# First pair's casts to GpSimd and copies to ScalarE, gate halves in two PSUM banks, and a newly listed order, in a block-sparse attention and MLP-mixer kernel

## Chip, cores, metric

One core of a Trainium2 chip. The metric is the device time in microseconds (us) of one execution, the median of several runs. Engines are named as in the profile: PE (TensorE), DVE (VectorE), ACT (ScalarE), POOL (GpSimd), SP (SyncE, here used only to issue DMAs).

## The reference

```python
# q, k, v: (4, 8, 768, 64) float32; block 64, so 12 blocks; top_k 3
k_rep = k.reshape(B, H, 12, 64, D).mean(axis=3)
gate  = einsum('bhsd,bhnd->bhsn', q, k_rep), -1e9 where the block lies in the future
# each query attends to the 3 best blocks and to its own block, causally
attn  = softmax(where(mask & causal, q @ k^T / 8, -1e9)) @ v
x  = attn as (B, S, 512)
h  = relu(x^T @ w_tok1) @ w_tok2 ;  u = x + h^T          # token mixing, 768 -> 256 -> 768
out = u + relu(u @ w_ch1) @ w_ch2                         # channel mixing, 512 -> 1536 -> 512
```

Inputs and output are float32; the kernel computes scores, attention and the MLP in float16 and the gate in float32.

## The kernel before, in words

The 32 heads are worked in 16 pairs, four pairs to a batch (`pair(p)`, p = 0 to 15), and after each batch's pairs stands its channel MLP (`mlp(b)`). For a pair:

- q and k are loaded ("k<-in_k_dram", "q<-in_q_dram", line 516; q from pair 6 on and k from pair 7 on in another layout, line 508), transposed on PE (line 446) or, later, on DVE (lines 539, 596). v is loaded by a DMA that POOL issues and that casts to float16 ("VA", line 525), as are the weights ("w", "wc", line 426).
- From the transposed k, DVE sums blocks (line 553, tile "ks") and `spread` (line 534) copies the sums to the two heads' places. PE multiplies them with the transposed q (line 639: the gate), DVE adds the causal bias (643), takes the top 8 (670), compares with the third (683) and clears the own block (690, tile "bn"). "bn" is transposed by PE (710) and stands as 12 further rows under q (tile "QA"), so that one matmul gives score and mask (731, tile "sc").
- QA's upper rows are q cast to float16; KA's are k cast to float16 (lines 342 and 344: `copy` on ACT, and on DVE or POOL).
- ACT takes the exponent (744, tile "E"), POOL clears the upper triangle (752), PE multiplies with v (761), DVE divides (764, 768). Token mixing follows: 779, 783 or 784, 793, 796, and u is transposed, on PE (807) for the first four pairs, and later by DVE and a trip through DRAM ("turn", lines 452, 456, 460). The channel MLP is lines 827 (first matmul), 835 and 837 (relu), 849 (second matmul), 853 and the store.

The first pair (`cut`, p < CUT = 1) is worked in two halves of the sequence, so that it can start when half of its data is there: its transposes, gates, "bn" and scores come in two parts.

The order of every engine's instructions is fixed while the kernel is recorded. `Plan` holds all steps with their costs by engine (in ns), their dependences and a priority each (`pr`, from the numbers in `L`); `Plan.run` lists them greedily, and also decides which engine takes a step that several could take. Each engine then runs its list strictly in order. Where the plan sees PE wait, `fill` puts in matmuls of zeros (line 899) until the first MLP step. Costs for DMAs are (issue, landing, transfer); `LANES` = 8 is how many SP and ACT transfers may be under way. `P.alone` names the PSUM rings whose tiles are used by one engine at a time: a step of another engine on the same tile waits for the earlier one.

Of the kernel before, what the change touches and what calls it, by code (L numbers as in the profile page):

```python
# [51 lines left out]
EARLY, PACE = 5.78, 16.48  # L52
L = dict(kd=28.39, qd=24.29, vd=11.04, kt=13.4, kr=28.62, ke=-12.17, qt=24.03, qe=-10.99, q16=7.68, g=11.64, b=22.27,
         k16=20.14, r=24.99, w1=-9.34, w2=-3.8, wc1=11.98, wc2=30.18, tok=11.05, ml=12.98, o0=-2.69, o1=2.1, o2=2.23,
         o3=-0.75, o4=-2.45, o5=-0.39, o6=-3.33, o7=-8.31, o8=-1.83, o9=0.42, o10=-4.09, o11=-5.38, o12=6.03,
         o13=-1.8, o14=0.66, o15=3.06, m0=-0.25, m1=4.0, m2=6.99, m3=2.31, th=5.48, bd=5.16, cu=0.88, cs=5.86,
         ua=3.23, ub=23.41, ku=26.38, k0=5.54, k1=3.72, qu=23.81, dq=5.5, qp=5.5, dk=6.49, va=-11.68, ekd=26.02,
         eqd=24.07, evd=9.12, ekt=15.03, ekr=34.55, eke=-11.24, eqt=24.03, eqe=-6.62, eq16=4.03, eg=11.13, eb=22.27,
         etok=17.72)
# [28 lines left out]
class Plan:  # L88
# [6 lines left out]
    DMA = 1.1  # L95
# [33 lines left out]
    def run(self, on_slot_end=None, fill=None):  # L129
        free = dict(FREE)  # L130
        dma_free, lanes = 0.0, [0.0] * self.LANES
# [30 lines left out]
        def start(o, e):  # L162
            t = max(free[e] + held(o, e), o.not_before)
            if ported(o, e):
                t = max(t, shared[0])
            if e in ("SP", "ACT") and len(o.cost[e]) > 2:
                t = max(t, lanes[0])
# [23 lines left out]
        while ready:  # L191
# [47 lines left out]
            if len(o.cost[e]) > 2:  # L239
                begin = max(dma_free, t + occ)  # L240
                dma_free = begin + o.cost[e][2] * self.DMA
                o.end = dma_free + lat
                if e != "POOL":
                    lanes.pop(0)
                    lanes.append(o.end)
# [54 lines left out]
def kernel(  # L300
# [122 lines left out]
    def weight(name, dst, src, n, each, pr, after):  # L423
        b = Buf(None)
        W[name] = (b, 0)
        P.op({"POOL": (800.0, 2200.0, n * each / 16.0)}, lambda: nc.gpsimd.dma_start(out=dst, in_=src), rd=[after], wr=[(b, 0)], pr=pr)

    def weights(after):
        weight("w1", w1, moe_w_tok1.rearrange("(j p) t -> p j t", p=128), 768, 60, L["w1"], after)
        weight("w2", w2, moe_w_tok2.rearrange("(g p) s -> p g s", p=128), 256, 135, L["w2"], after)  # L430
        for c in range(NCC):
            weight(("wc1", c), wc1[:, c, :], moe_w_ch1[128 * c:128 * c + 128, :], 128, 247, L["wc1"] + c, after)
        for f in range(0, NFC, 3):
            weight(("wc2", f), wc2[:, f:f + 3, :], moe_w_ch2[128 * f:128 * f + 384, :].rearrange("(g p) c -> p g c", p=128),
                   384, 98, L["wc2"] + f / 3, after)
# [46 lines left out]
    def pair(p):  # L482
# [38 lines left out]
        if p < 3:  # L521
# [3 lines left out]
        P.op({"POOL": (1100.0, 2200.0, 1536 * 16.0 / 16)}, lambda: nc.gpsimd.dma_start(  # L525
            out=VA.t[:, :, :, 0:64], in_=vs.rearrange("x (j p) d -> p x j d", p=128)), wr=[(VA, 0)], pr=t0 - lead["vd"], not_before=5000.0)

# [4 lines left out]
        def spread(e, z):  # L532
            for x in range(2):
                ENG[e].tensor_copy(out=ks2b.t[64 * x:64 * x + 64, x, z], in_=ks3.t[64 * x:64 * x + 64, 0, z])  # L534

        if straight_k:
# [6 lines left out]
            for x in range(2):  # L543
                P.op({"POOL": (772.0, 820.0), "ACT": (721.0, 825.0), "DVE": (470.0, 555.0)}, lambda e, x=x: copy(ENG[e], KA.t[0:64, x, :], KT.t[64 * x:64 * x + 64]),
                     port=True, rd=[(KT, 0), (KT, 1)], wr=[(KA, (x, 0)), (KA, (x, 1))], io=f"S{2 * x}>S0", pr=t0 - lead["ke"])
            if not thirds:
                P.op({"POOL": (380.0, 450.0), "DVE": (160.0, 240.0)}, lambda e: spread(e, slice(0, NB)), rd=[(ks3, 0), (ks3, 1)], wr=[(ks2b, 0), (ks2b, 1)], pr=t0 - lead["kr"] + 0.1, io="S0>S0 S2>S2")
        else:
            k16 = Buf(k16r)
            for i in range(2):  # L550
                t = Buf(Rr)
                P.op(pe(slow=3), lambda t=t, i=i: transposed(k32, i, t.t), rd=loaded(k32, i), wr=[(t, 0)], pr=at(i, lead["kt"]))
                P.op(dve(HS), lambda t=t, i=i: nc.vector.tensor_reduce(  # L553
                    out=ks3.t[:, 0, 6 * i:6 * i + 6], in_=t.t[:, 0:HS].rearrange("c (n w) -> c n w", w=64),
                    axis=AX.X, op=ALU.add), rd=[(t, 0)], wr=[(ks3, i)], io="P0>S0", pr=at(i, lead["kr"]))
                if not thirds and (cut or i == 1):
                    z = slice(6 * i, 6 * i + 6) if cut else slice(0, NB)
                    P.op({"POOL": (380.0, 450.0), "DVE": (160.0, 240.0)}, lambda e, z=z: spread(e, z), rd=[(ks3, i)] if cut else [(ks3, 0), (ks3, 1)],
                         wr=[(ks2b, i)] if cut else [(ks2b, 0), (ks2b, 1)], pr=at(i, lead["kr"]) + 0.1, io="S0>S0 S2>S2")
# [34 lines left out]
        for i in range(2):  # L594
# [9 lines left out]
            P.op({**act(HS), **dve(HS)}, qev, rd=[(t, 0)], wr=[(QT, i)], io="P0>S0", pr=at(i, lead["qe"]))  # L604
# [5 lines left out]
        if straight_q and thirds:  # L610
            P.op({"POOL": (1207.0, 1257.0), "DVE": (745.0, 828.0)}, lambda e: ENG[e].tensor_tensor(
                out=R1.t, in0=QT.t[:, 128:S], in1=upper(QT.t[:, 128:S]), op=ALU.subtract), port=True, rd=[(QT, 0), (QT, 1)], wr=[(R1, 0), (R1, 1)], io="S0>S0", pr=t0 - L["r"])
# [14 lines left out]
        g = Buf(Rr)  # L627
        gm, m8, bn = Buf(gmr), Buf(m8r), Buf(bnr)
        W2 = 2 * NB
        if not thirds:  # L630
            if cut:
                P.op({"POOL": (100.0, 150.0)}, lambda: nc.gpsimd.memset(gm.t[:, 0:2].rearrange("p j (x n) -> p j x n", n=NB)[:, :, :, 6:NB], -1.0e9), wr=[(gm, 9)], pr=t0 - lead["g"] - 9.0)
            for i, (z0, z1) in enumerate(parts):
# [3 lines left out]
                def gate(z0=z0, z1=z1, nb=nb):  # L637
# [4 lines left out]
                P.op(pe(slow=2 * (z1 - z0)), gate, rd=both_q + [(ks2b, 0)] + ([(ks2b, 1)] if z1 > 2 else []), wr=[(g, i)], pr=at(i, lead["g"]))  # L642
                P.op({"DVE": (200.0 * (z1 - z0) / 5 + 40.0 * cut, 290.0)}, lambda z0=z0, z1=z1, nb=nb, cols=cols: nc.vector.tensor_tensor(
                    out=cols(gm.t[:, z0:z1]), in0=g.t[:, W2 * z0:W2 * z1].rearrange("p (j w) -> p j w", w=W2)[:, :, 0:2 * nb].rearrange("p j (x n) -> p j x n", n=nb),
                    in1=cols(gbias[:, z0:z1]), op=ALU.add), rd=[(g, i)] + ([(gm, 9)] if cut else []), wr=[(gm, i)], io="P0S0>S0", pr=at(i, lead["g"]) + 0.1)
        else:
# [11 lines left out]
            for i in range(3):  # L658
                P.op({"DVE": (202.0, 283.0)}, lambda i=i: nc.vector.tensor_tensor(out=gm.t, in0=gv(2 - i), in1=(gm.t if i else gbias), op=ALU.add),
                     rd=[(g, 0)], wr=[(gm, 0)], io="P0S0>S0", pr=t0 - lead["g"] + 0.1)  # L660

        for i, (z0, z1) in enumerate(parts):
# [8 lines left out]
            P.op({"DVE": (730.0 * nz / 5, 730.0 * nz / 5 + 90.0)}, top, rd=[(gm, i)], wr=[(m8, i)], io="S0>S0", pr=at(i, lead["g"]) + 0.2)  # L671
            nb = 6 if cut and i == 0 else NB
            if thirds:
                P.op({"DVE": (92.0, 174.0)}, lambda z0=z0, z1=z1, third=third: nc.vector.tensor_copy(out=third(), in_=m8.t[:, z0:z1, :, 2:3]),
                     rd=[(m8, i)], wr=[(g, (3, i))], io="S0>P0", pr=at(i, lead["g"]) + 0.25)
                pair_of = lambda: (gm.t.rearrange("p j (x n) -> p j x n", n=NB), third())
            else:
                pair_of = lambda z0=z0, z1=z1, nb=nb: (
# [5 lines left out]
            P.op({"DVE": (190.0 * sm, 190.0 * sm + 82.0)}, less, rd=[(gm, i), (g, i), (g, (3, i)), (m8, i)], wr=[(bn, i)], io="P0S0>S0", pr=at(i, lead["g"]) + 0.3)  # L684
# [6 lines left out]
            P.op({"POOL": (270.0, 340.0), "DVE": (150.0, 220.0)}, mine, rd=[(bn, i)], wr=[(bn, i)], io=">S0 >S2", pr=at(i, lead["g"]) + 0.4)  # L691
# [251 lines left out]
```

## Time and profile before

| what | value |
|---|---|
| median of 3 runs | 246.92 us (246.72 to 247.88) |
| profiled execution | 246.32 us, span 244.6 us |
| granted TensorE clock | 1.0 |
| busy: PE, DVE, ACT, POOL | 97%, 70%, 66%, 52% of the span |
| DMA packets | 30.82 MB, mean 126 GB/s |
| first channel-MLP matmul on the chain | at 56.46 us |

The span is the profiled program's time on the core; 1.72 us of the execution lie around it. In lists of groups a line reads: line, engine, operation, output <- input, count, busy us, mean ns. In the timeline a row is start, duration, engine, line, operation, shapes, and in brackets the idle time before it and what ended it. Chain rows are start, duration, and whose work it was. In the kernel after, the same lines have numbers higher by 13 to 19.

### The profile page before, as it was taken

The numbers are of one execution on the slowest core, as the hardware profiler recorded it, in microseconds if no ns is written. First come the engines' busy times: TensorE is split into PE (matmuls) and PEld (weight loads), VectorE is DVE, ScalarE is ACT, GpSimd is POOL, SyncE is SP. The second block draws the span as 40 slices with busy tenths as digits, with TensorE's granted clock in tenths as the row PEclk, the third lists the DMA queues.
The fourth block names the chain that finished last, engine by engine and source line by source line (L and its number), as shares of the span: only waits on it lengthen the run. The fifth ranks groups of instructions, "written<-read, shape, count | busy, mean of one in ns | idle before, by whom it ended". The sixth has DMA issues, their size and how long they took to land.

```text
span 244.6 us, 6642 instructions
## 1 busy us (share of the span) xinstructions
PE 238.1 (97%) x2467; PEld 162.9 (67%) x2467; DVE 170.4 (70%) x546; ACT 160.6 (66%) x251; POOL 128.2 (52%) x263
## 2 busy tenths in 40 slices
PE   7799999999999999999999999999999999999995
PEld 7588878897656676567575666567755766554644
DVE  3889887877879999999999889968385632202112
ACT  3786978759587696788988675589724672360620
POOL 6188778878487583978796747676102110000000
DMA  8999999999899897879999899510213211112103
GB/s 158 201 203 215 207 171 182 173 132 177 133 83 168 158 148 142 186 150 178 161 138 168 186 166 126 151 53 3 64 46 111 79 32 46 43 43 86 46 18 110
DMA packets 124120, 30.82 MB, mean 126 GB/s; under 512 B 117652, under 2 KB 120596, under 8 KB 124088
## 3 DMA queue, kind: packets, MB, share of 16 engines
q1 hardware_dynamic: 94400, 22.89, 46.7%
q0 software_dynamic: 28064, 7.08, 32.8%
q10 hardware_dynamic: 1624, 0.43, 0.9%
q8 instruction: 19, 0.31, 0.6%
q14 instruction: 13, 0.11, 0.2%
HBM read 29.01 MB, written 8.45 MB: 153 GB/s over the span
## 4 chain that ended last, share of the span: by engine, by line
PE 91%; DMA 3%; DVE 3%; issue 0%; SPq 0%; POOL 0%; POOLq 0%
PE pm L827 26%; PE pm L849 25%; PE sc L731 14%; PE pm L761 9%; PE pm L779 4%; PE pm L793 4%; DMA k<-in_k_dram 3%; PE pm L639 2%; PE pm L654 2%; PE pm L446 2%; PE pm L710 1%; PE pm L899 1%; DVE ks L553 1%; DVE ks L534 1%; PE pm L807 1%; DVE m L670 1%
## 5 line engine op out<-in xcount | busy, mean ns | idle before, releaser
L744 ACT ACTIVATE E<-sc 128x1024 f16<-128x1024 f32 (+2 forms) x96 | 84.0, 917 | 22.7 <-PE sc L731 21.3
L827 PE MATMUL pm<-uT,wc 128*128 128x384 f16 x384 | 69.9, 326 | 0.0
L849 PE MATMUL pm<-wc,h 128*128 128x512 f16 (+2 forms) x312 | 68.8, 363 | 0.0
L752 POOL TENSOR_SCALAR_AFFINE_SELECT E<-E 128x256 f16<-128x256 f16 (+1 forms) x96 | 39.2, 416 | 43.2 <-ACT E L744 41.4
L835 ACT ACTIVATE h<-pm 128x384 f16<-128x384 f32 x71 | 34.5, 491 | 28.2 <-PE pm L827 28.0
L827 PEld LDWEIGHTS <-wc 128*128 128x128 f16 x384 | 36.0, 98 | 22.5
L731 PE MATMUL sc<-QA,KA 76*128 76x512 f16 (+3 forms) x264 | 48.2, 301 | 0.3 <-DVE QA L344 0.3
L849 PEld LDWEIGHTS <-h 128*128 128x128 f16 x312 | 28.4, 98 | 26.0
L853 DVE TENSOR_TENSOR os<-u,pm 128x512 f32<-128x512 f16 (+2 forms) x26 | 16.6, 640 | 33.9 <-PE pm L849 33.2
L731 PEld LDWEIGHTS <-KA 76*128 76x128 f16 x264 | 23.6, 98 | 14.5 <-issue 0.4
L761 PEld LDWEIGHTS <-E 128*128 128x128 f16 x672 | 24.9, 98 | 3.6
L761 PE MATMUL pm<-VA,E 128*128 128x65 f16 x672 | 26.1, 193 | 0.0
L796 DVE TENSOR_TENSOR u<-x,pm 128x384 f16<-128x384 f16 x32 | 16.5, 542 | 4.7 <-PE pm L793 4.7
L837 DVE TENSOR_SCALAR h<-pm 128x384 f16<-128x384 f32 x25 | 13.8, 554 | 8.5 <-PE pm L827 7.5
L768 DVE TENSOR_TENSOR x<-pm,rc 128x384 f16<-128x384 f32 x32 | 17.8, 555 | 0.9
L525 POOL DMA_DIRECT2D VA<-in_v_dram x16 | 16.8, 1051 | 0.4 <-issue 0.3
L793 PE MATMUL pm<-h,w 128*128 128x128 f16 x192 | 13.8, 219 | 0.0
L342 ACT COPY QA<-bnt 12x384 f16<-12x384 f16 x20 | 10.2, 508 | 5.3 <-DVE bnt L695 4.9
L670 DVE MAX8 m<-gm 128x8 f32<-128x12 f32 x160 | 13.2, 156 | 0.5
L779 PE MATMUL pm<-x,w 128*128 128x128 f16 x192 | 13.3, 219 | 0.0
L793 PEld LDWEIGHTS <-w 128*128 128x128 f16 x192 | 11.9, 98 | 1.9
L779 PEld LDWEIGHTS <-w 128*128 128x128 f16 x192 | 11.7, 98 | 2.0 <-DVE x L768 0.4
(79 smaller groups left out, 302.2 us busy)
## 6 DMA issues: line engine op xcount, KB each, us to landing
out_dram<-os SPq DMA_DIRECT2D x22, 256.0 KB, 2.5
q<-in_q_dram SPq DMA_DIRECT2D x42, 96.0 KB, 2.9
k<-in_k_dram SPq DMA_DIRECT2D x38, 96.0 KB, 3.8
VA<-in_v_dram POOLq DMA_DIRECT2D x16, 192.0 KB, 6.0
wc<-in_moe_w_ch_dram POOLq DMA_DIRECT2D x8, 384.0 KB, 6.6
k<-in_k_dram SPq DMA_DIRECT2D x12, 192.0 KB, 5.6
turn<-k SPq DMA_DIRECT2D x11, 192.0 KB, 2.1
uT<-turn SPq DMA_DIRECT2D x44, 48.0 KB, 2.0
```

Of the source, the lines that this page charges most:

```text
L525: P.op({"POOL": (1100.0, 2200.0, 1536 * 16.0 / 16)}, lambda: nc.gpsimd.dma_start(out=VA.t[:, :, :, 0:64], in_=vs.rearrange("x (j p) d -> p ...
L731: nc.tensor.matmul(out=s.t[:, at:at + 128 * m], lhsT=KA.t[:, x, 128 * kk:128 * kk + 128], rhs=QA.t[:, q0:q0 + m, x, :], start=True, stop=True)
L744: nc.scalar.activation(out=E.t[:, BASE[g_]:BASE[g_ + 1]], in_=s.t[:, 0:WIDTH[g_]], func=AF.Exp, scale=scale)
L752: nc.gpsimd.affine_select(out=o, in_=o, pattern=[[0, len(d)], [1, 128]], compare_op=ALU.is_ge, fill=0.0, base=0, channel_multiplier=-1)
L761: nc.tensor.matmul(out=t[:, jq, :], lhsT=E.t[:, cc:cc + 128], rhs=VA.t[:, x, kk, :], start=(kk == 0), stop=(kk == jq))
L768: P.op(dve(384), lambda a=a, rc=rc, x=x: nc.vector.tensor_tensor(out=xp.t[:, :, 64 * x:64 * x + 64], in0=a.t[:, 0:NJ * 65].rearrange("p (j ...
L779: nc.tensor.matmul(out=m1.t[:, 128 * t:128 * t + 128], lhsT=w1[:, j, 128 * t:128 * t + 128], rhs=xp.t[:, j, :], start=(j == 0), stop=(j == ...
L793: nc.tensor.matmul(out=m.t[:, 128 * j:128 * j + 128], lhsT=w2[:, t, 128 * (j0 + j):128 * (j0 + j) + 128], rhs=h1.t[:, t, :], start=(t == 0 ...
L827: nc.tensor.matmul(out=m.t[:, 0:HS], lhsT=wc1[:, c, 128 * f:128 * f + 128], rhs=uT.t[:, c].rearrange("p (a w) -> p a w", a=4)[:, :, 96 * i ...
L835: nc.scalar.activation(out=o, in_=w, func=AF.Relu)
L849: nc.tensor.matmul(out=m.t[:, 0:wide], lhsT=h2.t[:, f, 128 * jj:128 * jj + 128], rhs=wc2[:, f, w:w + wide], start=(f == 0), stop=(f == NFC ...
L853: P.op(dve(wide), lambda j=j, m=m, o=o, w=w, wide=wide: nc.vector.tensor_tensor(out=o.t[:, w:w + wide].rearrange("p (c d) -> p c d", d=128 ...
```

## The change

For the first pair: q's casts to QA go to POOL alone (before: DVE or ACT), k's copies to KA and q's copies out of PSUM to ACT alone (before: DVE or ACT). The two halves of its gate get a PSUM bank each (`gs`), before they shared one. Its v load is issued only after the second half of q is transposed (`rd=[(QT, 1)]`); for other pairs the v load stands later in the text but waits for nothing new. `spread` on DVE is now a reduction over one element instead of a copy. The plan's costs are changed: some DVE costs up, the port rule for DVE and POOL taken away for several copies, POOL's transfers given a time of preparation and a queue of their own that pushes transfers already sent, and DMAs issued after 13 us with a full queue 1.3 us more. The numbers in `L` and `EARLY` are new, a key `kr1` is added, and with all this every engine's list is another.

```diff
-EARLY, PACE = 5.78, 16.48
+EARLY, PACE = 5.56, 16.48
...
-    DMA = 1.1
+    DMA = 1.05
+    PREPARE, BEHIND = 1200.0, 1300.0
...
             if len(o.cost[e]) > 2:
-                begin = max(dma_free, t + occ)
-                dma_free = begin + o.cost[e][2] * self.DMA
-                o.end = dma_free + lat
-                if e != "POOL":
+                span = o.cost[e][2] * self.DMA
+                if t > 13000.0 and dma_free > t + 500.0:
+                    lat += self.BEHIND
+                if e == "POOL":
+                    begin = max(cast_free, t + occ + self.PREPARE)
+                    cast_free = begin + span
+                    o.end = cast_free + lat
+                    for x in sent:
+                        if x.end - 1600.0 > begin:
+                            x.end += span
...
-        P.op({"POOL": (1100.0, 2200.0, 1536 * 16.0 / 16)}, lambda: nc.gpsimd.dma_start(
-            out=VA.t[:, :, :, 0:64], in_=vs.rearrange("x (j p) d -> p x j d", p=128)), wr=[(VA, 0)], pr=t0 - lead["vd"], not_before=5000.0)
...
         def spread(e, z):
             for x in range(2):
-                ENG[e].tensor_copy(out=ks2b.t[64 * x:64 * x + 64, x, z], in_=ks3.t[64 * x:64 * x + 64, 0, z])
+                if e == "DVE":
+                    nc.vector.tensor_reduce(out=ks2b.t[64 * x:64 * x + 64, x, z], in_=ks3.t[64 * x:64 * x + 64, 0, z].rearrange("c (n w) -> c n w", w=1), axis=AX.X, op=ALU.add)
+                else:
+                    nc.gpsimd.tensor_copy(out=ks2b.t[64 * x:64 * x + 64, x, z], in_=ks3.t[64 * x:64 * x + 64, 0, z])
...
                 for x in range(2):
-                    def kev(e, t=t, i=i, x=x):
-                        copy(ENG[e], KA.t[0:64, x, halves(i)], t.t[64 * x:64 * x + 64, 0:HS])
-                    P.op({**dve(HS), **act(HS)}, kev, rd=[(t, 0), (ks3, i)] if cut else [(t, 0)], wr=[(KA, (x, i))], io=f"P{2 * x}>S0", pr=at(i, lead["ke"]))
+                    def kev(t=t, i=i, x=x):
+                        nc.scalar.copy(out=KA.t[0:64, x, halves(i)], in_=t.t[64 * x:64 * x + 64, 0:HS])
+                    P.op(act(HS), kev, rd=[(t, 0), (ks3, i)] if cut else [(t, 0)], wr=[(KA, (x, i))], io=f"P{2 * x}>S0", pr=at(i, lead["ke"]))
...
-            P.op({**act(HS), **dve(HS)}, qev, rd=[(t, 0)], wr=[(QT, i)], io="P0>S0", pr=at(i, lead["qe"]))
+            P.op(act(HS) if cut else {**act(HS), **dve(HS)}, qev, rd=[(t, 0)], wr=[(QT, i)], io="P0>S0", pr=at(i, lead["qe"]))
...
+        P.op({"POOL": (1100.0, 2800.0, 1536 * 14.0 / 16)}, lambda: nc.gpsimd.dma_start(
+            out=VA.t[:, :, :, 0:64], in_=vs.rearrange("x (j p) d -> p x j d", p=128)), rd=[] if p else [(QT, 1)], wr=[(VA, 0)], pr=t0 - lead["vd"], not_before=5000.0)
...
-                P.op({"DVE": (300.0, 380.0), "ACT": (410.0, 510.0)} if cut else {"POOL": (772.0, 820.0)} if p < L["qp"] else
-                     {"POOL": (772.0, 820.0), "ACT": (721.0, 825.0), "DVE": (470.0, 555.0)},
-                     q16, port=True, rd=[(QT, i)] if cut else [(QT, 0), (QT, 1)], wr=[(QA, (x, 0, i))], io=f"S{2 * x}>S0", pr=at(i, lead["q16"]))
+                P.op({"POOL": (430.0, 480.0)} if cut else {"POOL": (772.0, 820.0)} if p < L["qp"] else
+                     {"POOL": (772.0, 820.0), "ACT": (721.0, 825.0), "DVE": (870.0, 955.0)},
+                     q16, rd=[(QT, i)] if cut else [(QT, 0), (QT, 1)], wr=[(QA, (x, 0, i))], io=f"S{2 * x}>S0", pr=at(i, lead["q16"]))
...
-        g = Buf(Rr)
+        gs = [Buf(Rr) for _ in parts]
+        g = gs[0]
...
-                P.op(pe(slow=2 * (z1 - z0)), gate, rd=both_q + [(ks2b, 0)] + ([(ks2b, 1)] if z1 > 2 else []), wr=[(g, i)], pr=at(i, lead["g"]))
+                P.op(pe(slow=2 * (z1 - z0)), gate, rd=both_q + [(ks2b, 0)] + ([(ks2b, 1)] if z1 > 2 else []), wr=[(gs[i], i)], pr=at(i, lead["g"]))
```

What the new lists hold, as the two programs are built (this is order alone):

- SP before: first pair k, q, k, q by halves; then k1, q1, k2, q2, k3, k4, q3, q4, k5, q5, k6, q6, k7, q7 (the number is the pair). After: q, k, q, k; then q1, k1, q2, k2, k3, q3, k4, q4, k5, q5, k6, q6, k7. The first "turn" store comes before q7 in the after list, and behind q7 in the before list.
- POOL before: v0 ahead of everything else of the first pair. After: two casts of q0, v0, two casts of q0, two casts of q1, then the clearing of "bn" for the first pair's second part, then w_tok1.
- PE after: q0, k0, q0, [zeros], gate 0 first part, k0, [zeros], q1, "bn" 0 first part, gate 0 second part, ten score matmuls, k1, and so on. PE's matmuls are the same in number and shape but for zeros: 99 instead of 103.

More of the change, by code (lines that the diff above doesn't have):

```diff
@@ L165, in start @@
                 t = max(t, shared[0])
-            if e in ("SP", "ACT") and len(o.cost[e]) > 2:
-                t = max(t, lanes[0])
+            if e in ("SP", "ACT") and len(o.cost[e]) > 2 and lanes[0]:
+                t = max(t, lanes[0].end)
             t = max(t, o.base[e])
@@ L239, in run @@
             if len(o.cost[e]) > 2:
-                begin = max(dma_free, t + occ)
-                dma_free = begin + o.cost[e][2] * self.DMA
-                o.end = dma_free + lat
-                if e != "POOL":
+                span = o.cost[e][2] * self.DMA
[8 more added lines that the diff above has]
+                            x.end += span
+                            for y in x.outs:
+                                if y.wait == 0 and y.start is None:
+                                    opened(y)
+                    dma_free = max(dma_free, begin) + span
+                else:
+                    dma_free = max(dma_free, t + occ) + span
+                    o.end = dma_free + lat
                     lanes.pop(0)
-                    lanes.append(o.end)
+                    lanes.append(o)
+                    sent = sent[-11:] + [o]
             for b in o.bufs:
@@ L543, in pair @@
             for x in range(2):
-                P.op({"POOL": (772.0, 820.0), "ACT": (721.0, 825.0), "DVE": (470.0, 555.0)}, lambda e, x=x: copy(ENG[e], KA.t[0:64, x, :], KT.t[64 * x:64 * x + 64]),
-                     port=True, rd=[(KT, 0), (KT, 1)], wr=[(KA, (x, 0)), (KA, (x, 1))], io=f"S{2 * x}>S0", pr=t0 - lead["ke"])
+                P.op({"POOL": (772.0, 820.0), "ACT": (721.0, 825.0), "DVE": (870.0, 955.0)}, lambda e, x=x: copy(ENG[e], KA.t[0:64, x, :], KT.t[64 * x:64 * x + 64]),
+                     rd=[(KT, 0), (KT, 1)], wr=[(KA, (x, 0)), (KA, (x, 1))], io=f"S{2 * x}>S0", pr=t0 - lead["ke"])
             if not thirds:
-                P.op({"POOL": (380.0, 450.0), "DVE": (160.0, 240.0)}, lambda e: spread(e, slice(0, NB)), rd=[(ks3, 0), (ks3, 1)], wr=[(ks2b, 0), (ks2b, 1)], pr=t0 - lead["kr"] + 0.1, io="S0>S0 S2>S2")
+                P.op({"POOL": (380.0, 450.0), "DVE": (250.0, 330.0)}, lambda e: spread(e, slice(0, NB)), rd=[(ks3, 0), (ks3, 1)], wr=[(ks2b, 0), (ks2b, 1)], pr=t0 - lead["kr"] + 0.1, io="S0>S0 S2>S2")
         else:
@@ L658, in pair @@
             for i in range(3):
[L659 removed]
+                P.op({"DVE": (215.0, 295.0)}, lambda i=i: nc.vector.tensor_tensor(out=gm.t, in0=gv(2 - i), in1=(gm.t if i else gbias), op=ALU.add),
                      rd=[(g, 0)], wr=[(gm, 0)], io="P0S0>S0", pr=t0 - lead["g"] + 0.1)
@@ L690, in mine @@
                     ENG[e].memset(o, 0.0)
-            P.op({"POOL": (270.0, 340.0), "DVE": (150.0, 220.0)}, mine, rd=[(bn, i)], wr=[(bn, i)], io=">S0 >S2", pr=at(i, lead["g"]) + 0.4)
+            P.op({"POOL": (270.0, 340.0), "DVE": (200.0, 270.0)}, mine, rd=[(bn, i)], wr=[(bn, i)], io=">S0 >S2", pr=at(i, lead["g"]) + 0.4)
         bn_all = [(bn, i) for i in range(len(parts))]
```

48 lines of the change are left out of this document (25 added, 23 removed).

## The prediction

> **What bounds the kernel now.** I read the page's busy line first, then the chain that ended last, whole, and the stretch to 40 us of it; durations and waits come from the timeline. Chain rows are start, duration, whose work.
>
> ```profile
> PE 238.1 (97%) x2467; PEld 162.9 (67%) x2467; DVE 170.4 (70%) x546; ACT 160.6 (66%) x251; POOL 128.2 (52%) x263
> ```
>
> ```profile
> 4.15 5.64 DMA k<-in_k_dram
> ...
> 12.14 0.53 DVE ks L534
> ...
> 12.69 0.90 DVE ks L534
> ...
> 14.87 1.04 PE pm L639 x10
> ...
> 19.65 0.67 PE pm L761 x21
> ...
> 22.11 0.87 PE sc L731 x6
> ...
> 24.21 0.67 PE pm L779 x12
> ...
> 29.39 1.03 PE pm L639 x10
> ...
> 33.13 0.47 PE pm L710 x5
> ```
>
> ```profile
> 56.46 1.95 PE pm L827 x12
> ```
>
> PE is the bound: from 36 us to the last matmul the chain is PE's own work. Only the front, to 33 us, holds DMA and DVE pieces. PE's matmuls are the same in number and shape after the change, so only two things can alter the time: how much of PE's front is spent waiting (or on zeros), and whether the new order opens a wait after 33 us, where there is none now. "Faster" and "slower" below mean by over 0.5%, 1.23 us of the 246.92 us median, about what a measurement can tell from no change.
>
> **The change, part by part.** I follow the new lists through the front with these durations and set milestones against the old.
>
> ```profile
> 3.31 1.19 POOL L525 DMA_DIRECT2D VA<-in_v_dram  x1
> 4.64 0.63 ACTq L523 DMA_DIRECT2D KA<-indc  x1
> 5.33 0.96 ACT L342 CAST KA<-pm 64x384 f16<-64x384 f32 x2 [0.87 <-DVE ks L553]
> 5.41 0.34 DVE L534 COPY ks<-ks 64x6 f32<-64x6 f32 x2
> 6.38 0.55 DVE L344 CAST QA<-QT 64x384 f16<-64x384 f32 x1
> 6.85 0.54 DVE L553 TENSOR_REDUCE ks<-pm 128x6 f32<-128x384 f32 x1
> 7.78 0.39 DVE L670 MAX8 m<-gm 128x8 f32<-128x12 f32 x4
> 8.46 0.18 DVE L690 MEMSET bn<- 64x4 f16 x2
> 8.53 0.82 PE L639 MATMUL pm<-ks,QT 128*128 128x24 f32 x6 [0.71 <-DVE bn L683]
> 9.93 0.84 PE L446 MATMUL pm<-id,k 128*128 128x128 f32 x6 [0.35 <-DMA k<-in_k_dram]
> 10.61 0.83 PE L731 MATMUL sc<-QA,KA 76*128 76x256 f16 x10
> 11.79 0.82 POOL L344 COPY KA<-k 64x768 f16<-64x768 f16 x1 [0.19 <-DVE k L344]
> 12.14 1.44 DVE L534 COPY ks<-ks 64x12 f32<-64x12 f32 x2
> 12.18 0.52 PE L446 MATMUL pm<-id,q 128*128 128x128 f32 x3 [0.59 <-DMA q<-in_q_dram]
> 14.05 0.81 POOL L344 CAST QA<-QT 64x768 f16<-64x768 f32 x1 [0.49 <-ACT QT L342]
> 17.07 1.83 ACT L744 ACTIVATE E<-sc 128x1024 f16<-128x1024 f32 x2
> 18.10 0.48 DVE L534 COPY ks<-ks 64x12 f32<-64x12 f32 x2
> 18.92 0.47 PE L710 MATMUL pm<-id,bn 128*64 128x128 f16 x5
> 22.82 1.00 PE L899 MATMUL pm<-zero 128*128 128x120 f16 x16
> ```
>
> *Gate of the first pair, two banks.* k0 now comes second, so its sum starts on DVE at 5.3 us, when q0 used to leave PE; before, it ended by 5.41, where the spread starts, and so began at 5.41 - 0.54 = 4.87 or sooner. The second half's sum ends near 7.95, before 6.85 + 0.54 = 7.39. On DVE then follow the maxima (0.39), the spread (0.34), the compare (about as long as the clear) and the clear (0.18): done at 9.1, before 8.64. The old wait of the second gate part for the compare (0.71) was the shared bank; two banks end it. But PE's list now has the transposes of "bn" ahead of that gate part, and those wait for the clear. So the gate part starts at 9.45, not 8.53: the banks gain nothing, 0.9 us is lost. The first ten scores, which no longer stand behind k1's transposes (0.84), come at 10.3, before 10.61.
>
> *Copies and casts.* ACT is free at 4.64 + 0.63 = 5.27 and copies at 0.48 each, as it did. POOL's 64x384 cast isn't in the trace: between half of its 64x768 cast, 0.41, and DVE's 0.55. I take 0.43 (the same engine). Two casts after q0's first half (5.8) are done at 6.7, long before the scores. DVE is rid of its 0.55 casts. POOL's list then holds v0's issue, two casts of q0, two of q1 (0.81 each, from 9.85) and only then the clear for "bn"'s second part, done at 11.8. What hides it are k1's transposes, done at 11.8 if k1 lands at 11. If q1 landed as late as k1 did before (9.79), the clear would come at 13.2 and cost 1.4 us.
>
> *v0 later.* Its issue moves from 3.31 to about 7.0, behind q0's second half.
>
> ```profile
> 5.00:10.00 5.00, 3.47 (x33) 2.77 (x32) 4.38 (x23) 3.65 (x9) 0.00 (x0) 1.00 1.54 197
> ```
>
> ```profile
> q1 hardware_dynamic: 94400, 22.89, 46.7%
> q0 software_dynamic: 28064, 7.08, 32.8%
> ```
>
> ```profile
> VA<-in_v_dram POOLq DMA_DIRECT2D x16, 192.0 KB, 6.0
> ```
>
> v0 is 192 KB: 1.0 us at the 197 GB/s of that window (its last column), or by its queue's share 0.328 x 244.6 / 7.08 us per MB x 0.197 MB = 2.2 us. By so much the first load behind it, now q1, lands earlier than 9.79: 7.6 to 8.8, I take 8.0; k1, which shares the engines with v0, at 11.0, where q1 landed about 12.1. v0 itself, issued at 7.0 plus its 1.19, lands about 14; the first product with v comes at 17.8. It is hidden by over 3 us.
>
> *Spread as a reduction.* The chain shows 0.53 + 0.90 us for a spread that took 0.48 at 18.10; beside the 1.44 ran POOL's copy at 11.79. As a reduction it isn't in the trace: 0.48 to 1.44. I take 0.5: 0.48 is what the step takes where nothing holds it up. The Trainium skill (SBUF — State Buffer, Who interferes with whom) says that DVE copies can lock the port pair shared with GpSimd and that a reduction never does on this chip; the 1.44 beside POOL's copy agrees. By that rule 0.5 holds; if reductions were held up too, the sum would lose 0.9 us.
>
> *Second pair.* k1's transposes end at 11.8; sums, copy (0.54 each, one sum beside the transposes) and spread bring its gate to 13.9, before 14.87: 1.0 us. Before, DVE did two sums and a spread of the next pair between maxima and compare; the new list compares at once. From the gate's end to the transposes of "bn" it was 18.92 - (14.87 + 1.04) = 3.01; without 2 x 0.54 and 0.48 it is 1.45. With the gate ended at 13.9 + 1.04 = 14.95, "bn" is there at 16.4, not 18.92. Then ACT sets the pace: the exponents at 0.9 each and q's two copies between them end the first pair at 18.85, as before (17.07 + 1.83). The products with v, after POOL's masks, come no earlier than before: 17.8 and 20.35, the second where 19.65 stood. But the second pair's scores go ahead where PE ran 16 zeros (1.00): at the token step of pair 0, 24.2 both times, eight more score matmuls are done, as many as the row of six (0.87) and two more, 1.12 us. Worked on in the same way, pair 3's gate ends at 30.45, before at 29.39 + 1.03 = 30.42. By then the old list has caught up with those eight, but the new one has done three more scores (half of 0.87) and two products with v (0.67 each): 0.43 + 1.34 = 1.77 us ahead.
>
> *To 33 us.* Between pair 2's compare and pair 3's bias add DVE has some thirteen steps of 0.2 to 0.55; the add starts about 31.5, a microsecond after its gate, and "bn" is transposed at 33.4, before 33.13: 0.25 lost, 1.5 left. w_tok2, issued about 24.5 behind two v loads, lands (by v's 6.0, and up to 8 with three such transfers under way, an estimate) at 30.5 to 32.5, and PE wants it at 32.35: 0.2 off.
>
> *From there* I carry 1.3 us to the end: PE is as full in both lists. Sum against the profiled execution: 246.32 - 1.3 = 245.0 (span 243.3); the median lay 0.6 above that execution, so 246.92 - 1.3 = **245.6 us**.
>
> **The rivals.**
>
> *A. Nothing arrives (about 246.9).* The loads, not PE's list, set when the first channel MLP can start (56.46). For it: the DMA share in the window above is over 1. The skill's page DMA: Bandwidth & Descriptors (Queues, rings and completion order) has the engines take turns between queues; by that rule v0's cost is not removed, only moved to k1 and q2. Against: PE's waits for loads are small, 0.35 and 0.59 in the rows above, and none comes after 12.18. Here 1.3 is given back: 246.9, or 246.3 if half is.
>
> *B. Slower: pair 7's gate waits for q7.*
>
> ```profile
> 48.59 4.85 SPq L508 DMA_DIRECT2D q<-in_q_dram  x4
> ```
>
> ```profile
> 63.13 0.38 SPq L456 DMA_DIRECT2D turn<-k  x1
> ```
>
> ```profile
> 73.21 1.03 DVE L596 STREAM_TRANSPOSE QT<-q 128x384 f32<-128x384 f32 x2
> 74.27 0.87 DVE L611 TENSOR_TENSOR R<-QT 128x640 f32<-128x640 f32 x1
> ```
>
> ```profile
> 75.74 1.44 POOL L647 TENSOR_TENSOR R<-R 128x640 bf16<-128x640 f32 x1
> ```
>
> Before, q7's four loads were issued from 48.59. In the new list the first "turn" store stands ahead of them on SP, and it waits for pair 4's token step, which PE does just before its first MLP matmul: about 57.5. And PE wants pair 7's gate earlier, 15.7 us after that matmul, 71 us. Four issues as slow as then (4.85) end at 62.4; landing 5 us later, 67.4; transposes, remainder and second remainder (1.03 + 0.87 + 1.44), 70.8. That is just in time; each microsecond more is a microsecond of PE's. Landings of 9 us give 74.8, a stall of 3.8: 246.92 - 1.3 + 3.8 = 249.4. A stall over 2.5 us decides it. Against: the loads before it are fewer by then, and POOL's chain ahead of the second remainder is ready no earlier than 71 either, which alone may cost 0 to 1 us.
>
> *C. More.* k0's first half lands early enough for its transposes to stand where q0's did and its sum not to be late: the 0.9 us lost at the first pair's gate come back, 246.92 - 1.3 - 0.9 = 244.7.
>
> **How the numbers follow.** Forecast (245.0 to 246.2): 0.42, of which three fifths, 0.25, lie below 245.69, the bound of faster. A: 0.23, all within the bound. B, or another late wait of its size: 0.27. C: 0.08. Faster 0.25 + 0.08 = 0.33; same 0.17 + 0.23 = 0.40; slower 0.27. The range reaches from 244.4, just under C, to 248.6, inside B: some 0.04 lie below it and 0.15 above. Under the forecast alone it would be 245.0 to 246.2, the ends being 0.6 each way: what v0's 1.0 to 2.2 us and the cast's 0.41 to 0.55 leave open.
>
> **What would show it.** Right: spread rows of 0.5 us near 13.5; "bn" of the second pair on PE before 17.2; no zeros run of 16 near 23; q1's transposes near 8 and k1's near 11; the first MLP matmul near 55.2. Wrong: POOL's clear of "bn" after 12.5, PE rows of line 673 (the gate from pair 6 on) with idle time ahead of them, a first MLP matmul at 56.5 or later, or PE waiting for "uT" or "w".

## The result, and the profile after

The changed kernel takes 248.61 us (median of 22 runs, 247.05 to 249.04), the kernel before 247.22 us (22 runs beside them): ratio 1.0038, 95% interval 1.002 to 1.0057. It is slower by 0.4%, where 1.3 us of gain (245.6 us) was forecast. Measured again beside other kernels (experiment 5) it is 247.21 us, ratio 1.0042 (1.0015 to 1.0069).

The executions of every kernel here fall into groups by the granted clock (1.0, 0.993, 0.986 and lower, on average over the span), so a median depends on how large each group is; "at full clock" below is the median of the executions at 0.998 or more. The changed kernel takes 247.2 at full clock and 248.7 at 0.993 (9 and 13 of the 22 runs). The kernel before, in the 108 runs beside the experiments, takes 246.4 to 246.5 at full clock (39 runs), 246.9 to 247.0 at 0.993 (36), and 247.9 or more below that. So the change costs 0.7 us at full clock. The kernel before loses clock in more of its executions (69 of 108, against 17 of 34 of the changed one with experiment 5), but less by it: 0.5 us at 0.993, where the changed kernel loses 1.5.

The profiled execution of the changed kernel (248.8 us, span 247.1) is one of those at 0.993. First its timeline, in the stretch where the forecast lead was lost (rows of PE, DVE and POOL together, as in the prediction: start, duration, engine, line, operation, and in brackets the idle time before it and what ended it):

```profile
9.02 0.84 PE L461 MATMUL pm<-id,q 128*128 128x128 f32 x6 [0.66 <-DMA q<-in_q_dram]
11.37 0.82 PE L461 MATMUL pm<-id,k 128*128 128x128 f32 x6
14.10 1.19 PE L658 MATMUL pm<-ks,QT 128*128 128x24 f32 x10
17.21 0.47 PE L729 MATMUL pm<-id,bn 128*64 128x128 f16 x5
...
24.54 0.83 PE L798 MATMUL pm<-x,w 128*128 128x128 f16 x12
26.49 1.03 POOL L629 DMA_DIRECT2D VA<-in_v_dram  x1
26.78 2.17 DVE L359 COPY KA<-k 64x768 f16<-64x768 f16 x2
27.90 1.74 POOL L359 CAST QA<-QT 64x768 f16<-64x768 f32 x2
28.98 0.97 DVE L569 TENSOR_REDUCE ks<-pm 128x6 f32<-128x384 f32 x2
30.05 0.37 PE L918 MATMUL pm<-zero 128*128 128x120 f16 x4 [0.36 <-ACT k L357]
30.45 0.33 DVE L547 TENSOR_REDUCE ks<-ks 64x12 f32<-64x12 f32 x2
30.83 1.29 PE L658 MATMUL pm<-ks,QT 128*128 128x24 f32 x10 [0.41 <-DVE ks L547]
32.83 1.49 PE L798 MATMUL pm<-x,w 128*128 128x128 f16 x12
...
89.74 1.26 POOL L666 TENSOR_TENSOR R<-R 128x640 bf16<-128x640 f32 x1
89.87 1.91 DVE L359 CAST QA<-QT 64x768 f16<-64x768 f32 x1
92.30 1.46 PE L846 MATMUL pm<-uT,wc 128*128 128x384 f16 x8 [0.25 <-DVE h L856]
110.88 0.68 PE L780 MATMUL pm<-VA,E 128*128 128x65 f16 x16 [0.31 <-POOL E L771]
```

To 17 us it runs in the forecast's order, 0.2 to 1.0 us later than it. Then two copies of KA for pair 3 take 2.17 us on DVE, beside POOL's issue of a v load and two casts; the reductions behind them start at 28.98, and pair 3's gate at 30.83, where the kernel before had it at 29.39. PE has little to do from 29.7 to 30.8. What follows is in the stretches (busy time and instructions of PE, its weight loads, DVE, ACT and POOL, then granted clock, DMA share, GB/s):

```profile
29.00:31.00 2.00, 1.23 (x28) 0.96 (x24) 1.92 (x7) 1.48 (x3) 1.09 (x2) 1.00 1.16 214
31.00:33.00 2.00, 2.00 (x17) 1.64 (x18) 1.93 (x9) 1.40 (x2) 1.94 (x4) 0.88 1.72 198
33.00:35.00 2.00, 2.00 (x17) 1.55 (x15) 1.25 (x10) 1.16 (x2) 1.33 (x5) 0.50 1.65 200
35.00:36.00 1.00, 1.00 (x12) 1.00 (x11) 0.16 (x1) 0.71 (x1) 0.91 (x3) 0.54 1.78 197
```

PE is called busy, and its clock is halved for 3.4 us: by the means of these rows from 32.5 (0.88 over two microseconds) to 35.9 (0.54 over one). Twelve token matmuls take 1.49 us, where twelve of the same shape took 0.83 at 24.54. At half clock 3.4 us are worth 1.7 of PE's work at most, which is about the 1.5 us between the changed kernel's two groups. The table shows PE's lost time, which is the time less what the matmuls done by then take at full clock (their number from the stretches, each at its line's usual duration, and zeros counted as lost); "two parts" is experiment 13, in which PE's list is the old one.

| by (us) | before | after | experiment 4 | two parts (13) |
|---|---|---|---|---|
| 29 | 11.9 | 10.5 | 10.3 | 10.7 |
| 35 | 12.4 | 13.0 | 11.3 | 11.2 |
| 60 | 13.4 | 14.5 | 12.3 | 12.1 |
| 90 | 13.4 | 14.5 | 12.3 | 12.3 |
| 111 | 13.8 | 15.9 | 12.9 | 12.7 |
| 235 | 14.2 | 16.7 | 13.6 | 12.9 |

So the changed kernel was 1.4 us ahead at 29 us. It lost 2.5 from there to 35, 1.5 to 60 (the kernel before 1.0) and from 60 to 235 another 2.2, where the kernel before loses 0.8. Most of the 2.2 goes near 91 and 110, where DVE's QA cast of 1.91 us and POOL's late masks make PE wait; the three waits listed there come to 0.7 us.

Experiment 5's profile is an execution of the same program at full clock. Counted likewise from its trace, it is 1.5 us ahead of the kernel before at 29 us, 0.6 ahead at 35 and at 60, and 0.7 behind at 235, which is what the change costs at full clock.

### The profile page after: what moved, and what is told of

Same layout as the page of the kernel before. It is cut to its first block, busy times and chain, and to the rows that moved or that the text cites. A ratio compares the mean times of both kernels' runs of the same rounds, so it can differ in the third digit from the quotient of the medians.

```text
span 247.1 us, 6645 instructions
## 1 busy us (share of the span) xinstructions
PE 240.2 (97%) x2463; PEld 164.5 (67%) x2463; DVE 170.3 (69%) x545; ACT 161.2 (65%) x251; POOL 129.3 (52%) x264
## 4 chain that ended last, share of the span: by engine, by line
PE 81%; DVE 8%; DMA 3%; POOL 3%; issue 2%; ACT 2%; SPq 0%; DVEq 0%
PE pm L868 22%; PE pm L846 22%; PE sc L750 13%; PE pm L780 7%; PE pm L798 4%; PE pm L812 4%; DMA q<-in_q_dram 3%; PE pm L658 3%; PE pm L461 3%; PE pm L673 2%; ACT E L763 1%; DVE QA L359 1%; DVE h L856 1%; DVE KT L554 1%; POOL E L771 1%
## 5 line engine op out<-in xcount | busy, mean ns | idle before, releaser
L854 ACT ACTIVATE h<-pm 128x384 f16<-128x384 f32 x73 | 35.7, 491 | 26.2 <-PE pm L846 26.1
L750 PEld LDWEIGHTS <-KA 76*128 76x128 f16 x264 | 23.5, 99 | 13.8 <-issue 0.6
L780 PEld LDWEIGHTS <-E 128*128 128x128 f16 x672 | 25.4, 97 | 4.3 <-POOL E L771 0.7
L780 PE MATMUL pm<-VA,E 128*128 128x65 f16 x672 | 26.9, 193 | 0.5 <-POOL E L771 0.5
L359 POOL CAST QA<-QT 64x768 f16<-64x768 f32 (+1 forms) x18 | 13.9, 771 | 6.8 <-ACT QT L357 3.5
L357 ACT COPY QA<-bnt 12x384 f16<-12x384 f16 x19 | 9.7, 508 | 9.5 <-DVE bnt L714 9.3
L856 DVE TENSOR_SCALAR h<-pm 128x384 f16<-128x384 f32 x23 | 12.5, 548 | 4.0 <-ACT E L763 2.0
L798 PE MATMUL pm<-x,w 128*128 128x128 f16 x192 | 14.0, 225 | 0.1
L812 PEld LDWEIGHTS <-w 128*128 128x128 f16 x192 | 12.3, 100 | 2.1 <-issue 0.5
L798 PEld LDWEIGHTS <-w 128*128 128x128 f16 x192 | 12.3, 101 | 2.0 <-DVE x L787 0.5
```

The source lines that it names most:

```text
L750: nc.tensor.matmul(out=s.t[:, at:at + 128 * m], lhsT=KA.t[:, x, 128 * kk:128 * kk + 128], rhs=QA.t[:, q0:q0 + m, x, :], start=True, stop=True)
L780: nc.tensor.matmul(out=t[:, jq, :], lhsT=E.t[:, cc:cc + 128], rhs=VA.t[:, x, kk, :], start=(kk == 0), stop=(kk == jq))
L798: nc.tensor.matmul(out=m1.t[:, 128 * t:128 * t + 128], lhsT=w1[:, j, 128 * t:128 * t + 128], rhs=xp.t[:, j, :], start=(j == 0), stop=(j == ...
L812: nc.tensor.matmul(out=m.t[:, 128 * j:128 * j + 128], lhsT=w2[:, t, 128 * (j0 + j):128 * (j0 + j) + 128], rhs=h1.t[:, t, :], start=(t == 0 ...
L854: nc.scalar.activation(out=o, in_=w, func=AF.Relu)
```

## The experiments

All change single steps of the finished lists and plan nothing anew. `num[n]` is step n of the plan, `put(n, m)` moves it directly behind step m, and a third argument gives it to another engine.

**1. Pair 3's KA copies out of the way** (`e1_ka_later`).

```diff
     order = P.run(on_slot_end, fill)
+    put(369, 143)    # KA copies of pair 3, behind pair 0's "h"
+    put(370, 369)
+    put(223, 222)    # pair 4's cast of k, behind pair 3's spread
```

> The changed kernel with three steps of VectorE's list moved and nothing else: pair 3's two "KA" copies (k16 to KA, 64x768) go from ahead of its gate's reductions to behind pair 0's bias step "h", where VectorE idles (33.9 to 35.8 us in the changed kernel), and pair 4's cast of k goes behind pair 3's spread. In the changed kernel those two copies hold VectorE from 26.78 to 28.95 us, pair 3's gate starts at 30.83, PE has run dry before it, and the granted clock is halved from 33 to 35.5. Theory 1 (the two copies, 0.90 and 1.26 us long instead of the 0.35 that I took, cost the front its lead): the gate starts at 29.4 to 29.8, PE has no gap over 0.4 us before it, no slice shows a clock under 1.0, the first MLP matmul comes by 56.0, and the time is 1.0 (the later gate) + 1.45 (the clock) below the 248.6 of the changed kernel: about 246.2. Rival 2 (loads or a later step would have stopped PE anyway): the gate is earlier, the first MLP matmul isn't, 248.0 or more. Rival 3 (the clock falls by itself, without regard to the gap): gate early, clock still 0.5 near 33 in about half the executions, median about 247.5.

246.63 us (12 runs), ratio to before 0.9989 (0.997 to 1.0009); 11 of 12 executions are at full clock, at 246.63. The gate starts at 29.75, and the two copies take 0.77 us together where they now stand:

```profile
28.87 0.82 PE L780 MATMUL pm<-VA,E 128*128 128x65 f16 x21
29.54 0.37 PE L918 MATMUL pm<-zero 128*128 128x120 f16 x4
29.75 1.25 PE L658 MATMUL pm<-ks,QT 128*128 128x24 f32 x10
...
33.61 0.77 DVE L359 COPY KA<-k 64x768 f16<-64x768 f16 x2
```

Against experiment 5 at full clock (247.08) the earlier gate is worth 0.45 us, not the 1.0 expected; the clock's 1.5 us is saved in all but one execution. PE then waits for POOL's clear of "bn" (0.33 us, experiment 4), which takes some of it.

**2. The same wait, filled** (`e2_av_twice`).

```diff
+    order.insert(order.index(num[139]) + 1, num[139])   # 21 products with v, done twice
```

> The changed kernel with pair 2's 21 products with v ahead of pair 3's gate done twice (the same result written twice, 0.67 to 0.84 us of PE's time), nothing else: PE's wait for "ks" is left as it is and only filled. Theory 1 (the gap of about 1.1 us of PE before pair 3's gate makes the clock fall for 3.4 us): the gate still starts at 30.8, but the clock stays at 1.0, so the first MLP matmul comes at 56.7 instead of 58.17 and the time is about 247.2 in nearly all executions instead of 248.6 in most. Rival (the clock falls for another reason: load, a fixed time, chance): clock 0.5 near 33 to 35 in about half of the executions again, median 248.6 with the same two groups.

247.05 us, ratio 0.9977 (0.9945 to 1.001), 12 of 12 executions at full clock. The gate still waits for "ks", and the clock stays up:

```profile
30.72 1.29 PE L658 MATMUL pm<-ks,QT 128*128 128x24 f32 x10 [0.27 <-DVE ks L547]
33.00:35.00 2.00, 2.00 (x29) 1.56 (x26) 1.83 (x10) 1.97 (x3) 1.33 (x5) 1.00 1.73 207
```

The changed kernel has 17 of 34 executions at full clock (9 of 22, and 8 of 12 in experiment 5). More work, though useless, keeps the clock: here it is the idle time that lets it fall, not the load. At full clock nothing changes (247.06 against 247.08), as it should.

**3. Two late casts** (`e3_late`).

```diff
+    put(733, 614, "POOL")   # QA cast at 89.87, from DVE to POOL's idle time
+    num[868].eng = "DVE"    # KA cast at 104.91, from POOL to DVE
```

> The changed kernel with two casts on another engine, both after 88 us: one QA cast that took VectorE 1.91 us at 89.87 beside GpSimd's subtraction goes to GpSimd's idle time at 92.9, and one KA cast that took GpSimd 0.82 at 104.91, ahead of masks for which PE waits at 108.3 and 110.9, goes to VectorE, idle from 106.2. Theory (PE's late losses against the kernel before, 0.5 us near 91 and 0.85 us from 108 to 111, come from these two): 0.8 to 1.2 us below the changed kernel, 247.6 where it has 248.6 with the lowered clock. Rival (PE is held up by the next thing in the queue, exponents on ScalarE or GpSimd's next masks): less than 0.3 gained.

246.29 us, ratio 0.9989 (0.9963 to 1.0014): 246.26 at full clock (8 of 12), 247.80 in the other four, which keep the front's gap. Against 247.08 that is 0.8, the lower end of what was expected. The wait near 91 is gone; of those near 110 one of 0.31 stays.

**4. Both** (`e4_both`: the edits of 1 and 3).

> The first and the third experiment in one kernel. If the losses are separate, the gains add: 246.2 - 1.0 = 245.2 us, which is faster than the kernel before by 0.8%. If the front's lead only turns into a later wait, 246.9.

245.93 us, ratio 0.9959 (0.9938 to 0.9979). The gains nearly add: 0.45 + 0.8 against 1.2 at full clock (245.89). It is faster than before, but by less than the front's parts should give.

**5. The changed kernel again** (`e5_after_again`), unchanged.

> The changed kernel itself once more, in the same company as the next three, to hold them and the first four against. If the gap of PE before pair 3's gate is what lets the clock fall, then it falls in a good part of the executions here (4 of 12 in the third experiment, which keeps the gap; 2 of 36 in those that close or fill it): 4 to 8 of 12, and the median lies at 247.3 or at 248.7, whichever group is larger. If the lowered clock came from the place of the first measurement, all executions lie near 247.2.

247.21 us, 8 of 12 at full clock (247.08), four lower (248.4 to 250.2). With experiment 3 and the first measurement, kernels that keep the gap have 25 of 46 executions at full clock; experiments 1, 2 and 4, which close or fill it, 34 of 36.

**6. v0's load first again** (`e6_v0_first`), in the kernel of experiment 4.

```diff
+    order.remove(num[24])
+    order.insert(0, num[24])   # v0's load, issued at 3.26 us
```

> The kernel of the fourth experiment (KA copies later, two late casts on other engines; 245.9 us) with v0's load issued first on GpSimd's queue again, as before the change; nothing else. Theory (v0's transfer was what q1 and k1 waited behind): q1's transposes start 1.0 to 1.5 us later than its 9.0, k1's likewise, the second pair's gate and everything to 30 us is later by 0.7 to 1.0, and the time is 246.6 to 246.9. Rival (the engines share all queues, so that v0 behind q1 only takes from k1 and q2 what it gave to q1): q1 0.5 later, the second pair's gate and the end within 0.2 us: 245.9.

249.53 us, ratio 1.0068 (1.0034 to 1.0101); 247.26 in the two executions at full clock. q1 lands 1.6 us later than in experiment 4, where its transposes start at 8.84, and PE stands still for it; first experiment 4's row, then two of this one:

```profile
8.84 0.84 PE L461 MATMUL pm<-id,q 128*128 128x128 f32 x6 [0.35 <-DMA q<-in_q_dram]
```

```profile
10.42 0.85 PE L461 MATMUL pm<-id,q 128*128 128x128 f32 x6 [1.85 <-DMA q<-in_q_dram]
12.78 0.82 PE L461 MATMUL pm<-id,k 128*128 128x128 f32 x6
```

1.4 us arrive at the end, where 0.7 to 1.0 was expected, and ten of twelve executions lose clock besides. The rival, by which engines share all queues, falls. The prediction's price for this transfer, 1.0 to 2.2 us, was right.

**7. Spreads as copies again** (`e7_spread_copies`), in the kernel of experiment 4: `tensor_reduce` in `spread` back to `tensor_copy`.

> The kernel of the fourth experiment with VectorE's spreads as copies again instead of reductions, in the same places; nothing else. Theory (copies of VectorE between parts of the memory are held up by what GpSimd does beside them, reductions are not): spreads of 12 columns cost 0.2 to 1.4 us instead of 0.16 each, those of the first two pairs above all, because GpSimd casts and issues loads beside them; the second pair's gate is 0.3 to 1.0 us later and the time 0.2 to 0.8 more than 245.9: 246.1 to 246.7. Rival (the form doesn't matter where the order is this one): spreads of 0.2, the same time within 0.2.

247.27 us, ratio 1.0019 (1.0002 to 1.0036), all at full clock: 1.4 us lost, where 0.8 was the most expected. Its rows show where it starts:

```profile
6.47 0.61 DVE L547 COPY ks<-ks 64x6 f32<-64x6 f32 x2
9.07 0.33 DVE L547 COPY ks<-ks 64x6 f32<-64x6 f32 x2
13.56 0.69 DVE L547 COPY ks<-ks 64x12 f32<-64x12 f32 x2
```

The first and the third stand beside casts, issues and masks of POOL; the second, with POOL idle, takes what a reduction takes (0.33 at 30.45 in the changed kernel, 0.30 to 0.32 in experiment 4). Three later ones, up to 49 us, take 0.66 to 1.11, against 0.33 or 0.34 in experiment 4.

**8 and 9. Pair 3's clear of "bn" on DVE**, in the kernel of experiment 4: in `e8_clear_dve` at its old place in the list, which is behind the moved copies, and in `e9_clear_first` right behind the compare.

```diff
+    num[237].eng = "DVE"        # experiment 8
+    put(237, 236, "DVE")        # experiment 9
```

> The kernel of the fourth experiment with pair 3's clear of "bn" on VectorE instead of GpSimd, where it started 0.3 us after its compare and PE waited 0.33 us for it. Theory: the five transposes of "bn" and all behind them come 0.3 us earlier, 245.6 us. Rival: pair 0's bias step, now behind the clear on VectorE, delays the token mixing by as much: 245.9.

> The kernel of the fourth experiment (245.9 us) with pair 3's clear of "bn" on VectorE right behind its compare. In the eighth experiment the same clear stood behind pair 0's bias step and two KA copies and PE waited 1.52 us; here it stands ahead of them. Theory: PE's wait of 0.33 us for the clear goes, no clock is lost, 245.6 us. Rival: the bias step, 0.2 us later, gives it to the token mixing and to PE: 245.9.

Both miss. Experiment 8: 248.83 us (6 runs), ratio 1.011 (1.0063 to 1.0157), no execution at full clock; DVE's order, which the expectation overlooked, puts the clear behind two copies, and PE waits 1.52 us. Experiment 9: 246.73 us, ratio 0.9985 (0.9968 to 1.0003), 0.8 slower than experiment 4. The clear comes early, but the copies behind it now meet POOL's masks:

```profile
33.65 1.61 POOL L771 TENSOR_SCALAR_AFFINE_SELECT E<-E 128x256 f16<-128x256 f16 x4
34.30 1.18 DVE L359 COPY KA<-k 64x768 f16<-64x768 f16 x2
35.51 1.02 DVE L815 TENSOR_TENSOR u<-x,pm 128x384 f16<-128x384 f16 x2
36.12 0.55 PE L461 MATMUL pm<-id,q 128*128 128x128 f32 x3 [0.96 <-DVE u L815]
```

The two copies that took 0.77 in experiment 1 take 1.18 here, 0.7 us later, and PE waits 0.96 us for the step behind them. (This gap lost no clock in 12 executions.)

**10, 11, 12. Parts of the change in the old list.** In `e10_before_v0` v0's load waits behind a small copy of q0; in `e11_before_spread` `spread` is the new one; `e12_before_two` has both.

```diff
+    hold.fn = lambda: nc.gpsimd.tensor_copy(out=tiny, in_=QTr.tiles[0][0:64, 0:64])
+    put(10, 22)                                  # v0's load, behind q0's first copy ...
+    order.insert(order.index(num[10]), hold)     # ... and behind this one on POOL
```

> The kernel before with one part of the change alone: v0's load waits on GpSimd's queue until q0's first half has been copied (a 64x64 copy into a scratch tile ahead of it, about 0.2 us), so that it is issued at 6.5 instead of 3.3 us. Theory (v0's transfer costs the loads behind it 1.5 us, as the sixth experiment showed in the new list): k1's transposes at 8.5 instead of 9.93, q1's at 10.7 instead of 12.18, the second pair's gate 0.8 to 1.2 us earlier, PE ahead by as much at 33 us; in executions at full clock 245.3 instead of 246.4. Rival (in the old list VectorE's spread beside GpSimd's copy, 1.44 us at 12.14, and the first pair's casts set the second gate): less than 0.3 gained.

> The kernel before with the other part alone: VectorE's spreads as reductions. Theory: the spread at 12.14 takes 0.35 instead of 1.44 us, but its gate then waits for q1's transposes, which end at 13.3 and are copied by 13.9, so that only 0.3 to 0.6 of the 1.1 us arrives: 245.9 at full clock. Rival (all of it arrives): 245.3. Rival (nothing, q1 sets it): 246.4.

> The kernel before with both parts, the rest of its list unchanged. If the change's gain in the front comes from these two, and its loss from the rest of the new list, then this is faster than the changed kernel by far: 1.1 + 0.6 and some 0.4 that each alone leaves to the other below 246.4 at full clock, 244.4 to 244.8. If the old list can't use the lead (it was ordered for late loads: zeros, then masks and exponents at their old places), 245.5 to 246.

| | median, runs | at full clock | ratio to before |
|---|---|---|---|
| v0 later | 247.63, 12 | 246.15 (2) | 1.0025 (0.9993 to 1.0057) |
| spread as reduction | 246.76, 12 | 245.74 (3) | 0.9981 (0.9961 to 1.0001) |
| both | 244.68, 7 | 244.65 (4) | 0.9917 (0.9888 to 0.9947) |

Full clock before, beside these: 246.46. At full clock the parts alone give 0.3 and 0.7 (from two and three executions), together 1.8. In experiment 10 two spreads beside POOL's work still take 0.56 and 0.59 us, where experiment 12 has 0.32 and 0.33:

```profile
7.42 0.56 DVE L534 COPY ks<-ks 64x6 f32<-64x6 f32 x2
12.14 0.59 DVE L534 COPY ks<-ks 64x12 f32<-64x12 f32 x2
```

That isn't the 1.44 of before, and this profile has the clock halved from about 10 us; what else keeps the gain at 0.3 is not shown. In experiment 11 PE still waits for k1:

```profile
9.97 0.84 PE L446 MATMUL pm<-id,k 128*128 128x128 f32 x6 [0.78 <-DMA k<-in_k_dram]
```

Together no wait of PE for a load is left in the profile of experiment 12, and after its start only this one in its list of waits (in all, times, longest):

```profile
PE pm L642 <- DVE bn L686: 0.7, 1, 0.7
```

Experiment 13's profile, at full clock, has two waits for loads again, 0.48 us at 5.78 and 0.54 at 16.95. In experiment 12's profile, one of the three executions with a lowered clock, the clock falls at about 9.8 us, 1.3 us after this wait:

```profile
10.00:13.00 3.00, 3.00 (x21) 2.47 (x20) 2.20 (x9) 2.33 (x4) 1.56 (x4) 0.50 1.81 189
```

**13. The two parts, and this wait filled** (`e13_two_filled`).

```diff
+    z = next(o for o in order[order.index(num[23]):] if o.n == -1)
+    order.insert(order.index(z), z)      # seven zeros become fourteen
```

> The kernel of the twelfth experiment (the kernel before with v0's load later and the spreads as reductions) with the seven zeros ahead of the second gate part doubled, so that PE's wait of 0.69 us for the compare at 8.5 is filled to 0.2; nothing else. There 4 of 7 executions took 244.6 to 244.7 at a granted clock of 1.0 and 3 of 7 took 246.1 or more at 0.993 or less, with the clock halved between 10 and 13 us. Theory (idle time of PE of 0.7 us and more in the first 40 us is what lets the clock fall, 1.45 us each time): full clock in at least 10 of 12 executions, median 244.7, faster than the kernel before and than the changed one by 0.9%. Rival (the clock falls by the load of the other engines or by chance): full clock in about half, median between 244.7 and 246.1.

244.73 us, ratio 0.9914 (0.9884 to 0.9944), 6 of 6 executions at 0.998 or more. It is the fastest version whose executions all keep the clock (experiment 14, with the same zeros, keeps it in 7 of 7), 2.2 us under the kernel before as measured beside it:

```profile
6.90 0.90 PE L902 MATMUL sc<-zero 128*128 128x120 f16 x14
8.11 0.82 PE L642 MATMUL pm<-ks,QT 128*128 128x24 f32 x6 [0.32 <-DVE bn L686]
```

**14. The part that the change is named for** (`e14_named_part`), in the kernel of experiment 13.

```diff
+    put(10, 37)                     # v0's load, behind two casts instead of the small copy
+    for n in (35, 37, 36, 38):
+        num[n].eng = "POOL"
+    num[22].eng = "ACT"
```

> The kernel of the thirteenth experiment with the part of the change that its name tells: the first pair's four casts on GpSimd (before: two on VectorE, two on ScalarE) and its first copy of q on ScalarE (before: VectorE), in the old list; v0's load stands on GpSimd's queue behind two of these casts, as in the changed kernel, instead of behind the 64x64 copy. Theory (this part is neutral: its casts are done long before the first scores): 244.7 again, within 0.2. Rival 1 (GpSimd's casts hold up VectorE's copies or push its clear of "bn" back): 245.0 to 245.5, and this part would be one of those that cost the changed kernel its gain. Rival 2 (VectorE, rid of 1.1 us of casts, brings the second gate part earlier): 244.2 to 244.5.

245.05 us, ratio 0.9922 (0.9893 to 0.9951), all 7 at full clock. That is 0.3 more than experiment 13, inside the spread of both (244.5 to 245.5): neutral, or a small loss at the low end of what the first rival expected. POOL's casts take 0.53 each (1.06 for two), and its clear of the first pair's "bn" isn't late. But PE waits for pair 3's clear, which it doesn't in experiment 13's profile; whether that is the 0.3 was not tested:

```profile
32.10 0.47 PE L713 MATMUL pm<-id,bn 128*64 128x128 f16 x5 [0.45 <-POOL bn L693]
```

## Why the prediction was wrong

*Right: the front's gain and where it comes from.* The price of v0's transfer (1.0 to 2.2) is 1.6 in experiment 6. Its rule for the spread holds too: 0.30 to 0.33 as a reduction, 0.69 as a copy in experiment 7. The Trainium skill (SBUF — State Buffer, Who interferes with whom) says that VectorE's copies can be locked out by GpSimd and its reductions never; these rows agree. q1 landed at 9.0, not 8.0, and the front's other milestones ran 0.2 to 0.8 us late, but PE was 1.4 ahead at 29 us, where 1.77 was forecast for pair 3's gate.

*Wrong: the step "To 33 us".* It said that DVE has "some thirteen steps of 0.2 to 0.55" there, let 0.25 be lost and carried 1.5 on. By 35 us 0.9 of the lead is gone at full clock (experiment 5), and all of it where the clock falls. Two of these steps were KA copies ahead of the gate's reductions. The changed kernel's own group shows their range (least, median, most, in ns):

```profile
L359 DVE COPY KA<-k x6: 519/556/1261, 13.7 to 63.7; 64x768 f16<-64x768 f16 x6
```

They took 0.90 and 1.26 us. I had used the rule that GpSimd's work holds up VectorE's copies for the spread and not for the other copies of the same list, though the kernel before has the same form at 0.82, beside POOL's cast of 14.05:

```profile
14.25 0.82 DVE L344 COPY KA<-k 64x768 f16<-64x768 f16 x1
```

The gate's delay itself costs 0.45 us (experiment 1).

*Missed: the clock.* The prediction treats PE's waits as time lost once. Here the wait costs 1.5 us more in half of the executions (17 of 34; none of 12 where it is filled, experiment 2). The quoted profile of before could not show this, being an execution at full clock.

*Wrong: "PE is as full in both lists"* from 33 us on. From 60 us the new list loses 1.4 us more than the old (2.2 against 0.8 in the table), in waits of 0.2 to 0.3 (DVE's cast of 1.91 us, POOL's masks behind a cast); 0.8 of it comes back by moving two casts (experiment 3).

*The rivals.* A, that nothing arrives because loads set the MLP's start, is refuted by experiment 12, where 1.8 us arrive at the end; and in experiment 6 k1 comes as much later as q1 (12.78 against 11.20), so that v0's cost is not only moved from one load to the next. B was on the right side for another reason: pair 7's gate never waited for q7. C did not happen. The signs given ahead for "wrong" show it: POOL's clear of "bn" ended at 12.6, and the first MLP matmul came at 58.2.

*The sum at full clock.* The two parts take 246.46 to 244.65. The named part adds 0 to 0.3, pair 3's copies 0.45, the late casts 0.8; with 245.0 + 1.2 = 246.2 against 247.1 measured, some 0.9 us stays open. What is left for it, the rest of the new order and the two gate banks, was not tried apart.

## What to carry to other kernels

Cost a VectorE copy by what GpSimd does beside it, wherever a list places it, and put the step that PE waits for ahead of such copies or write it as a reduction. Fill PE's short waits with zeros, since a wait may cost more afterwards than while it lasts. Try the parts of a change in the old list before planning a new one: here two of them were worth 1.8 us, and the new list took back 2.5.

## What was not expected of the hardware

In the profiled execution a gap of 1.1 us on PE, with 0.37 us of zeros in it, was followed by 3.4 us at half clock. Kernels with this gap have a lowered clock in 21 of 46 executions and full clock in the others; the same program does either. The Trainium skill (TensorE: Matmul & The Clock Gate, Part 1) has a free-running window of about 3.4 us, which agrees with the length and would fit the chance, but asks for a whole idle window before the clock falls; here about a third of one was enough. No threshold follows: the 0.96 us of experiment 9 cost no clock.
